# A later load for the last four token tiles, and one z2 tile moved ahead of the second group's q, k chunks

## The chip, the cores and the metric

The kernel runs on one core of a Trainium2 chip. Its time is the device time of one execution in microseconds (us). TensorE (PE) multiplies matrices, VectorE (DVE), ScalarE (ACT) and GpSimd (POOL) work on tiles in the on-chip memory, SyncE (SP) issues transfers. Each engine takes its own list of instructions in order and waits on semaphores for the others.

## The reference

The input x has 2048 tokens of 512 values (bf16). Two branches read the same layer-normed tokens, and their results are added to x.

```
xn = layernorm(x)
# branch A: 32 heads of 16 values; each token attends to itself and the 7 tokens 2, 4, .. 14 places back
q, k, v = split(xn @ wqkv)
attn = softmax(q . k[pos - 2 w] / 4, w = 0..7)
A = (sum_w attn[w] * v[pos - 2 w]) @ wo
# branch B: gated MLP that mixes the tokens
z = gelu(xn @ w_in)            # 1376 columns
z1, z2 = z[:, :688], layernorm(z[:, 688:])
g = w_sp @ z2 + b_sp           # 2048 x 2048 over the tokens
B = (z1 * g) @ w_out
out = x + A + B
```

## The kernel before

The tokens are 16 tiles of 128. Nearly all data stays on chip; the order of the work is written out by hand in two lists of short names, `vec` (VectorE, and what hangs on it) and `ten` (TensorE, and the ScalarE work behind it). `advance` walks through both and calls `do` for each name, after what `needs` demands of the other list. Every engine then works off its own instructions in the order in which `do` made them. DMA issues of SP stand in one queue in the order of the calls.

What the names around the change mean, with the lines of the profile:

- `s` (L184, L185) are the mean and variance of a token tile, `r` (L188, L189) its 1/sigma on GpSimd, `n` (L198) the normed tile on VectorE, `t` (L207) its turn: a transpose by DMA on SP's queue into `xnT`, for tiles 4 to 15. Tiles 0 to 3 are turned on TensorE (`T`, L203).
- `LX` calls `load_tokens`: tokens of tiles 8 to 11 and of tiles 12 to 15, in two transfers (L143) of 512 KB from SP, each behind a memset of one word (L174) that ties its issue to VectorE's place in the list. Tiles 4 to 7 and the weights of q and k were issued before (`LE`).
- `k` with two digits is one of four chunks of q and k for a group of four token tiles (L256 on TensorE, copied by ScalarE at L258): k10, k12, k11 and k13 are those of the second group, tiles 4 to 7, and need the turns t4 to t7.
- `z` (L211) is the matmul of one tile of z2, `h` (L222) its gelu with a running sum on ScalarE, `q` (L227) its sum of squares on ScalarE. A tile z4 or later needs its own turn only.
- `zs` (L233 to L237) makes mean and 1/sigma of z2 for four tiles at once: three small steps on VectorE and then two on GpSimd (L236, and the power -1/2 at L237). `zn` (L243) norms one z2 tile on VectorE.
- `m` and `j` (L291) are products of q with a shifted k on VectorE; m00 is the first half of the first such product and j00 its other half, which needs k13. `f` (L294), `p` (L295) and the fold by DMA `d` (L300) add them up over a head's values, and `S` (L307) ends the sum on TensorE. `K` copies a border of k. `LW` loads the weights of v and z1 from GpSimd's queue.
- `v` (L271) are the values, `W` loads a part of w_sp (L369), `M` (L376) is the token mixing, 512 matmuls in all, and the output products (L414, L420, L426, L563) end the kernel.

The front of `vec` runs tile by tile; from tile 5 on each step is `s r` of a tile and then `n t` of the tile before it:

```
front = "s0 R0 LE s1 R1 V0 n0 V1 n1 s2 r2 s3 r3 n2 n3 LX s4 r4"
for i in range(5, NT):
    front += f" s{i} r{i} n{i - 1} t{i - 1}"
```

The q, k chunks and z2 tiles share three buffers in PSUM (`mm`), taken in turn.

Of the kernel before, what the change touches and what calls it, by code (L numbers as in the profile page):

```python
# [38 lines left out]
def kernel(  # L39
# [13 lines left out]
    V = nc.vector  # L53
# [46 lines left out]
    z2 = z2_r[:].rearrange("p (i f) -> p i f", i=NT)  # L100
# [5 lines left out]
    xs = z1_r[:, 0:NT * D].rearrange("p (i d) -> p i d", i=NT)  # L106
# [10 lines left out]
    def nxt(kind, pool):  # L117
        t = pool[count[kind] % len(pool)]
        count[kind] += 1
        return t  # L120
# [21 lines left out]
    def load_x(i, n=1):  # L142
        SP.dma_start(xs[:, i:i + n, :], x2[i * P:(i + n) * P, :].rearrange("(i p) d -> p i d", p=P))  # L143
# [26 lines left out]

    def load_tokens():

        for i in (8, 12):
            V.memset(xs[:, i, 0:2], 0.0)  # L174
            load_x(i, 4)

    def load_weights():
        G.dma_start(w_v, wq_d[:, :, 2 * D:3 * D])
# [21 lines left out]
    def turn_pe(i):  # L200
        pt = nxt("aux", aux)[:].bitcast(BF16)[:, 0:D]
        for c in range(C):
            PE.transpose(pt[:, c * P:(c + 1) * P], xn[i % 8][:, c * P:(c + 1) * P], ident[:])  # L203
        A.copy(xnT[:, :, i * P:(i + 1) * P], pt.rearrange("p (c t) -> p c t", c=C))  # L204

    def turn_dma(i):
        SP.dma_start_transpose(xnT[:, :, i * P:(i + 1) * P], xn[i % 8])  # L207

    def z_half(i, part, pz, hh):
        for kc in range(C):  # L210
            PE.matmul(pz[:, hh, 0:FHALF], xnT[:, kc, i * P:(i + 1) * P],  # L211
                      w_z2[:, hh, kc] if part else w_z1[:, kc, hh * FHALF:(hh + 1) * FHALF],
                      start=(kc == 0), stop=(kc == C - 1))

    def z_part(i, part):
        pz = nxt("mm", mm)
        for hh in range(2):
            z_half(i, part, pz, hh)
        return pz

    def z2_gelu(i, pz):
        A.activation(z2[:, i, :].rearrange("p (a b) -> p a b", a=2), pz[:, :, 0:FHALF],  # L222
                     ACT.Gelu_apprx_tanh, accum_out=zsum[:, i:i + 1])

    def z2_square(i):

        A.activation(z2_junk[:], z2[:, i, :], ACT.Square, accum_out=zsq[:, i:i + 1])  # L227
# [3 lines left out]
    def z2_stats(i, n):  # L231
        s = slice(i, i + n)
        V.tensor_scalar(zmean[:, s], zsum[:, s], 1.0 / FH, None, ALU.mult)  # L233
        V.tensor_tensor(zvar[:, s], zmean[:, s], zmean[:, s], ALU.mult)
        V.scalar_tensor_tensor(zvar[:, s], zsq[:, s], 1.0 / FH, zvar[:, s], ALU.mult, ALU.subtract)
        G.tensor_scalar(zvar[:, s], zvar[:, s], EPS, 1.0, ALU.add, ALU.mult)  # L236
        G.tensor_tensor(zrstd[:, s], zvar[:, s], mhalf[:, 0:n], ALU.pow)  # L237

    def z2_norm(i, on_act):
        if on_act:  # L240
            A.activation(z2[:, i, :], z2[:, i, :], ACT.Identity, bias=zbias[:, i:i + 1], scale=zrstd[:, i:i + 1])
        else:
            V.tensor_scalar(z2[:, i, :], z2[:, i, :], zmean[:, i:i + 1], zrstd[:, i:i + 1],  # L243
                            ALU.subtract, ALU.mult)
# [5 lines left out]
    def qk_chunks(b, a, c2):  # L250
        pq = nxt("mm", mm)
        t0 = b * D
        for cc in range(2):
            w_c = (w_k if a else w_q).rearrange("p k (o c) -> p k o c", c=C)[:, :, :, 2 * c2 + cc]
            for kc in range(C):
                PE.matmul(pq[:, cc, :], w_c[:, kc], xnT[:, kc, t0:t0 + D], start=(kc == 0), stop=(kc == C - 1))  # L256
        o = HALO + (b % 2) * D
        A.copy(qk[b // 2][:, a, 2 * c2:2 * c2 + 2, o:o + D], pq[:])  # L258
# [16 lines left out]
    def v_halo():  # L275
        G.dma_start(vp[H:P, :, :, 0:HALO], vp[0:P - H, :, :, GS:GS + HALO])
        G.dma_start(vp[0:H, :, 1, 0:HALO], vp[P - H:P, :, 0, GS:GS + HALO])
# [166 lines left out]

    front = "s0 R0 LE s1 R1 V0 n0 V1 n1 s2 r2 s3 r3 n2 n3 LX s4 r4"
    for i in range(5, NT):
        front += f" s{i} r{i} n{i - 1} t{i - 1}"
    front += " n15 t15"
    vec = front.split() + """
        zs0 LW m00 j00 zn0 zn1 zn2 zn3 f00 p00 K m01 d01 m02 d02 zs4 m03 d03 zn4 zn5 zn6 zn7  # L450
        p01 p02 zs8 m10 zn8 zn9 zn10 zn11 p03 W1 f10 zs12 p10 zn12 zn13 zn14 zn15
        m11 d11 g0 x0 m12 d12 p11 g1 u0 m13 p12 W2 W3 f13 p13 c0 g2
        a0.0 a0.1 g3 x1 a0.2 a0.3 g4 a0.4 g5 a0.5 a0.6 a0.7 g6 u1 a0.8 g7 a0.9 g8 a0.10 g9 a0.11 c1 g10
        a1.0 a1.1 g11 a1.2 a1.3 g12 a1.4 g13 a1.5 g14 a1.6 a1.7 g15 X1 a1.8 a1.9 F0 a1.10 a1.11 F1 F2
    """.split()
    ten = """
        T0 T1 GL z0 z1 h0 T3 h1 z2 h2 z3 h3 k00 k01 q0 k02 k03 q1 q2 q3 k10 k12 k11 k13
        W0 k20 z4 h4 q4 k21 z5 h5 q5 k22 z6 h6 q6 k23 z7 h7 q7 k30 z8 h8 q8 k31 z9 h9 q9 S00 v0
        k32 z10 h10 q10 k33 z11 h11 q11 z12 h12 z13 h13 q12 v1 S01 S02 v2 z14 h14 q13 z15 h15 q14 v3
        q15 v4 B S03 y0 y1 M0 S10 v5 v6 EL v7 H e0 M1 EG y2 y3 y4 EL1 i0 EG1 M2 y5 y6 y7 y8 y9 S11 S12 S13 M3 y10 y11 M4 y12  # L460
        M5 W4 W5 y13 y14 y15 O4 EL2 e1 M6 O0 O1 M7 W6 i1 M8 O2 M9 W7 M10 O3 M11 M12 X0 M13 M14 M15 Q0 Q2 Q3
    """.split()
# [115 lines left out]
    def do(n):  # L578
        k, a = n[0], n[1:]
        i = int(a) if a.isdigit() else 0  # L580
        th, w2 = (int(a[0]), int(a[1])) if len(a) == 2 and a.isdigit() else (i, 0)
        if k == "T":
            turn_pe(i)
        elif n[:2] == "zs":
            z2_stats(int(n[2:]), 4)
        elif n[:2] == "zn":
            z2_norm(int(n[2:]), False)
        elif n == "z0":

            gates["z0"], gates["z1"] = nxt("mm", mm), nxt("mm", mm)  # L590
            for t, hh in ((0, 0), (1, 0), (0, 1)):
                z_half(t, 1, gates[f"z{t}"], hh)
        elif n == "z1":
            turn_pe(2)
            z_half(1, 1, gates["z1"], 1)
        elif k == "z":
            gates[n] = z_part(i, 1)
        elif k == "h":
            z2_gelu(i, gates[f"z{i}"])
        elif k == "q":  # L600
            z2_square(i)
        elif k == "k":
            qk_chunks(th, w2 // 2, w2 % 2)
        elif k == "v":
            v_pair(i)
        elif k == "H":
            v_halo()
        elif k == "S":
            head_sum(th, w2)
        elif k == "B":  # L610
            pb = nxt("aux", aux)[:].bitcast(BF16)[:, 0:NT]
            PE.transpose(pb, b16[:], ident[0:NT, 0:NT])
            A.copy(b_col[:], pb)
        elif k == "y":
            z1_tile(i)
        elif k == "M":
            gates[i] = mix_tile(i)
        elif k == "W":
            load_wsp(i)
        elif k == "O":  # L620
            load_wo(i) if i < 4 else load_wout()
        elif k == "X":
            load_res(i)
        elif n == "GL":
            A.preload_act_table(ACT.Gelu_apprx_tanh)
        elif n[:2] == "EG":
            A.preload_act_table(ACT.Gelu_apprx_tanh)
        elif n[:2] == "EL":
            A.preload_act_table_set("natural_log_exp_and_others")
        elif k == "Q":  # L630
            [out_pair, None, lambda: out_group(2), lambda: out_last(3)][i]()
        elif k == "F":
            if i == 0:
                finish_pair(groups[i][0])
                finish_pair(groups[i][2])
            else:
                for t in groups[i]:
                    finish(t, po[t])
        elif k == "e":
            softmax_exp(i)  # L640
        elif k == "i":
            softmax_inv(i)
        elif k == "s":
            ln_stats(i)
        elif k == "R":
            ln_root_act(i, 1)
        elif k == "V":
            ln_inv(i)
        elif n == "LE":
            load_early()  # L650
        elif k == "r":
            ln_root(i, 1)
        elif k == "n":
            ln_norm(i)
        elif k == "t":
            turn_dma(i)
        elif n == "LX":
            load_tokens()
        elif n == "LW":
            load_weights()  # L660
        elif k == "m":
            run(prod_ops(th, w2)[0])
        elif k == "j":
            run(prod_ops(th, w2)[1])
        elif k == "f":
            prod_ops(th, w2)[2]()
        elif k == "p":
            prod_ops(th, w2)[3]()
        elif k == "d":
            fold_dma(th, w2)  # L670
        elif k == "K":
            k_halo()
        elif k == "x":
            run(softmax_max(i))
        elif k == "u":
            run(softmax_sum(i))
        elif k == "c":
            run(softmax_scale(i))
        elif k == "g":
            gate(i, gates[i])  # L680
        elif k == "a":
            at[int(a[0])][int(a[2:])]()
        done.add(n)

    def run(ops):
        for f in ops:
            f()
# [48 lines left out]
```

## Time and profile before

| | |
|---|---|
| median of 3 runs | 202.96 us (202.73 to 204.01) |
| profiled execution | 203.05 us, its span 201.3 us |
| TensorE busy | 194.7 us, 1575 matmuls |
| VectorE busy | 176.1 us |
| ScalarE busy | 95.9 us |
| GpSimd busy | 38.8 us |
| transfers | 30.84 MB, 153 GB/s in the mean |

The span goes from the first to the last instruction that the profile shows; the time holds some 1.8 us around it. A busy share says what an engine does over the whole span; what decides is which engine waits for which at one place, and the chain of work that ended last tells it. In a timeline a row is: start, length, engine, line, operation, output and inputs with their shapes, the count, and in brackets the idle time of the engine before it with what ended it.

### The profile page before, as it was taken

To read this page: it belongs to the slowest core of one execution; us is meant where nothing else is said; L and a number is where in the kernel's file an instruction comes from. 1 tells how busy PE (TensorE), PEld (TensorE's weight loads), DVE (VectorE), ACT (ScalarE), POOL (GpSimd) and SP (SyncE) were. 2 spreads that over 40 slices of the span, in tenths; PEclk is the share of its full clock that TensorE was granted. 3 is DMA by queue.
4 is the path that set the end of the run, shared out by engine and by line. 5 is a ranking of instruction groups with operands and counts; after the bars stand their busy time and mean duration, and the time that the engine had idled before them with its cause. 6 is when DMAs were issued, how large, how long until landed. Compare 5 with 4: busy or idle time off the path is not lost.

```text
span 201.3 us, 3826 instructions
## 1 busy us (share of the span) xinstructions
PE 194.7 (97%) x1575; PEld 117.7 (58%) x1583; DVE 176.1 (87%) x193; ACT 95.9 (48%) x149; POOL 38.8 (19%) x62
## 2 busy tenths in 40 slices
PE   6898999999999999999999999999999999999993
PEld 2554555555666666666566666666666664444652
DVE  4868989999799799999999999989999799897233
ACT  3778869998989349786443165311122110000000
POOL 2355773139460430700000000000000000000000
PEclk9999999999999999999999999999999999999999
DMA  5996649999941939995978099997989411722023
GB/s 143 357 283 113 83 104 211 209 139 218 212 99 26 185 65 142 202 112 121 209 171 170 0 241 299 188 232 128 267 119 273 92 39 40 237 81 100 8 104 104
DMA packets 64353, 30.84 MB, mean 153 GB/s; under 512 B 53504, under 2 KB 62576, under 8 KB 64208
## 3 DMA queue, kind: packets, MB, share of 16 engines
q1 hardware_dynamic: 59808, 19.76, 48.9%
q0 software_dynamic: 1904, 6.59, 17.2%
q10 hardware_dynamic: 2624, 4.25, 8.3%
q8 instruction: 12, 0.20, 0.4%
q14 instruction: 5, 0.04, 0.1%
HBM read 10.03 MB, written 2.10 MB: 60 GB/s over the span
## 4 chain that ended last, share of the span: by engine, by line
PE 89%; DMA 6%; DVE 3%; POOL 1%; issue 1%
PE mm L376 37%; PE mm L211 16%; PE mm L256 10%; PE mm L271 7%; PE mm L414 7%; PE mm L426 5%; DMA z<-in_A_x_dram 4%; PE aux L414 2%; PE mm L563 1%; DVE stats L184 1%; DMA xnT<-z 1%; PE mm L420 1%; PE aux L307 1%; DVE z L198 1%; POOL rstd L189 1%
## 5 line engine op out<-in xcount | busy, mean ns | idle before, releaser
L376 PE MATMUL mm<-z,wsp 128*128 128x344 bf16 x512 | 75.8, 309 | 0.0
L376 PEld LDWEIGHTS <-wsp 128*128 128x128 bf16 x512 | 49.9, 98 | 25.2 <-issue 0.8
L211 PE MATMUL mm<-wts,xnT 128*128 128x344 bf16 x256 | 40.4, 310 | 0.2 <-ACT xnT L204 0.2
L379 ACT ACTIVATE qk<-mm,b_col 128x688 bf16<-128x688 f32 x16 | 13.3, 833 | 50.6 <-PE mm L376 50.6
L349 DVE TENSOR_TENSOR prod<-vp,a_sb 128x4096 bf16<-128x4096 bf16 x16 | 36.1, 2285 | 0.0
L211 PEld LDWEIGHTS <-xnT 128*128 128x128 bf16 x256 | 24.6, 98 | 13.9 <-issue 0.6
L256 PE MATMUL mm<-xnT,wts 128*128 128x512 bf16 x123 | 28.8, 380 | 0.8 <-DMA xnT<-z 0.6
L291 DVE TENSOR_TENSOR prod<-qk 128x4096 bf16<-128x4096 bf16 (+1 forms) x14 | 27.1, 1980 | 0.3 <-PE aux L307 0.3
L353 DVE TENSOR_TENSOR prod<-prod,prod 128x8192 bf16<-128x8192 bf16 x6 | 26.5, 4421 | 0.1
L256 PEld LDWEIGHTS <-wts 128*128 128x128 bf16 x128 | 14.3, 114 | 13.4 <-issue 1.8
L258 ACT CAST qk<-mm 128x1024 bf16<-128x1024 f32 x16 | 16.1, 1011 | 5.2 <-PE mm L256 5.2
L271 PE MATMUL mm<-xnT,wts 128*32 128x512 bf16 x256 | 14.8, 381 | 0.0
L414 PE MATMUL mm<-wts,qk 128*128 128x512 bf16 (+1 forms) x62 | 14.2, 371 | 0.4 <-issue 0.3
L184 DVE BATCH_NORM_STATS2 stats<-z 128x6 f32<-128x512 bf16 x16 | 10.9, 683 | 3.9 <-DMA z<-in_A_x_dram 3.9
L248 ACT ACTIVATE z<-mm 128x688 bf16<-128x688 f32 x16 | 11.8, 743 | 4.8 <-PE mm L211 4.7
L414 PEld LDWEIGHTS <-qk 128*128 128x128 bf16 x85 | 8.1, 98 | 9.2 <-issue 0.6
L431 DVE TENSOR_TENSOR z<-mm,wsp 128x512 bf16<-128x512 f32 (+1 forms) x9 | 5.7, 657 | 8.0 <-PE mm L426 4.8
L227 ACT ACTIVATE z_junk<-z 128x688 bf16<-128x688 bf16 x16 | 12.4, 777 | 0.3
L222 ACT ACTIVATE z<-mm 128x688 bf16<-128x688 f32 x16 | 11.9, 744 | 1.5 <-PE mm L211 1.5
L271 PEld LDWEIGHTS <-wts 128*32 128x32 bf16 x256 | 9.5, 139 | 4.4 <-issue 0.6
L300 POOL DMA_DIRECT2D prod<-prod x8 | 7.1, 928 | 19.4 <-DVE prod L291 19.4
L426 PE MATMUL mm<-wts,xnT 32*128 32x512 bf16 x160 | 10.7, 375 | 0.0
(92 smaller groups left out, 184.6 us busy)
## 6 DMA issues: line engine op xcount, KB each, us to landing
prod<-prod POOLq DMA_DIRECT2D x8, 512.0 KB, 6.9
wts<-in_A_wo_dram ACTq DMA_DIRECT2D x4, 512.0 KB, 5.5
z<-in_A_x_dram SPq DMA_DIRECT2D x3, 512.0 KB, 6.6
out_dram<-z SPq DMA_DIRECT2D x11, 128.0 KB, 1.7
wts<-in_A_wqkv_dram SPq DMA_DIRECT2D x2, 512.0 KB, 6.0
z<-z POOLq DMA_DIRECT2D x2, 512.0 KB, 8.6
wsp<-in_A_x_dram ACTq DMA_DIRECT2D x1, 1024.0 KB, 5.4
wsp<-in_A_x_dram SPq DMA_DIRECT2D x1, 1024.0 KB, 5.3
```

Source lines behind the costliest of these rows:

```text
L184: V.bn_stats(stats[:, i, :], xs[:, i, :])
L211: PE.matmul(pz[:, hh, 0:FHALF], xnT[:, kc, i * P:(i + 1) * P], w_z2[:, hh, kc] if part else w_z1[:, kc, hh * FHALF:(hh + 1) * FHALF], star ...
L256: PE.matmul(pq[:, cc, :], w_c[:, kc], xnT[:, kc, t0:t0 + D], start=(kc == 0), stop=(kc == C - 1))
L258: A.copy(qk[b // 2][:, a, 2 * c2:2 * c2 + 2, o:o + D], pq[:])
L271: PE.matmul(pv[32 * g:32 * g + 32, dd, :], w, r, start=(kc == 0), stop=(kc == C - 1), tile_position=(0, 32 * g))
L291: ops.append(lambda ww=ww, k=k, c=c: V.tensor_tensor(pr[:, ww, c], q[:, c], k[:, c], ALU.mult))
L349: return lambda: V.tensor_tensor(dst, vp[:, :, th, off:off + GS], a_sb[:, th, w].unsqueeze(1).broadcast_to([P, DH, GS]), ALU.mult)
L353: return lambda: V.tensor_tensor(dst, dst, x, ALU.add)
L376: PE.matmul(pg[:, hh, 0:FHALF], w[:, k, (j % 2) * P:(j % 2 + 1) * P], z2[:, k, hh * FHALF:(hh + 1) * FHALF], start=(k == 0), stop=(k == NT ...
L379: A.activation(g.rearrange("p (a b) -> p a b", a=2), pg[:, :, 0:FHALF], ACT.Identity, bias=b_col[:, j:j + 1])
L414: PE.matmul(po[:, cols], uT[th][:, m, t0:t0 + P], wout[:, m, cols], start=(start and m == 0), stop=(stop and m == MF - 1))
L426: PE.matmul(pos[g], op[32 * g:32 * g + 32, th, d, s * P:(s + 1) * P], wo_r[32 * g:32 * g + 32, d, :], start=(start and d == 0), stop=(stop ...
```

## The change

The load of tokens 12 to 15 leaves `load_tokens`, with its memset, and becomes a step of its own, `LZ`, right behind t7 on SP. In `ten`, z4 with its gelu comes between q1 and q2, ahead of k10; the squares q2 and q3 are spread between the chunks, and z5 to z13 stand one place earlier than their forerunners. In `vec`, zn0 to zn3 come ahead of j00.

```diff
     def load_tokens():
-        for i in (8, 12):
-            V.memset(xs[:, i, 0:2], 0.0)
-            load_x(i, 4)
+        V.memset(xs[:, 8, 0:2], 0.0)
+        load_x(8, 4)
...
     for i in range(5, NT):
-        front += f" s{i} r{i} n{i - 1} t{i - 1}"
+
+        front += f" s{i} r{i} n{i - 1} t{i - 1}" + (" LZ" if i == 8 else "")
...
-        zs0 LW m00 j00 zn0 zn1 zn2 zn3 f00 p00 K m01 d01 m02 d02 zs4 m03 d03 zn4 zn5 zn6 zn7
+        zs0 LW m00 zn0 zn1 zn2 zn3 j00 f00 p00 K m01 d01 m02 d02 zs4 m03 d03 zn4 zn5 zn6 zn7
...
-        T0 T1 GL z0 z1 h0 T3 h1 z2 h2 z3 h3 k00 k01 q0 k02 k03 q1 q2 q3 k10 k12 k11 k13
-        W0 k20 z4 h4 q4 k21 z5 h5 q5 k22 z6 h6 q6 k23 z7 h7 q7 k30 z8 h8 q8 k31 z9 h9 q9 S00 v0
-        k32 z10 h10 q10 k33 z11 h11 q11 z12 h12 z13 h13 q12 v1 S01 S02 v2 z14 h14 q13 z15 h15 q14 v3
+        T0 T1 GL z0 z1 h0 T3 h1 z2 h2 z3 h3 k00 k01 q0 k02 k03 q1 z4 h4 q2 k10 k12 q3 k11 k13
+        W0 q4 k20 z5 h5 q5 k21 z6 h6 q6 k22 z7 h7 q7 k23 z8 h8 q8 k30 z9 h9 q9 k31 z10 h10 q10 S00 v0
+        k32 z11 h11 q11 k33 z12 h12 q12 z13 h13 q13 v1 S01 S02 v2 z14 h14 z15 h15 q14 v3
...
+        elif n == "LZ":
+            load_x(12, 4)
```

## The prediction

> **What bounds the kernel now.** The page first, for the busy shares; then the chain of work that ended last, for the places where the end does not hang on TensorE; then the timelines of VectorE and GpSimd from 5 to 67 us, for the slack behind these places.
>
> ```profile
> span 201.3 us, 3826 instructions
> PE 194.7 (97%) x1575; PEld 117.7 (58%) x1583; DVE 176.1 (87%) x193; ACT 95.9 (48%) x149; POOL 38.8 (19%) x62
> ```
>
> TensorE works 97% of the span, its clock row is 9 throughout, and the edit adds and removes no matmul. So the change can only open or close waits of TensorE, of which there are 6.6 us. The chain says which of them matter:
>
> ```profile
> 9.06 6.57 DMA z<-in_A_x_dram
> 15.65 0.70 DVE stats L184
> 16.35 0.02 issue
> 16.38 0.19 DVE mv L185
> 16.57 0.08 issue
> 16.64 0.24 POOL rstd L188
> 16.88 2.33 DMA xnT<-z
> 19.22 0.14 issue
> 19.35 4.27 PE mm L256 x19
> ```
>
> The reader is to see one loop: tokens 8 to 11, issued at 9.06, land at 15.62. Statistics of tile 8 (s8) wait for them, and the norm of tile 7 (n7) stands behind s8 on VectorE. So turn t7 is issued at 16.88 and lands at 19.2, and only then k10 (q, k chunks of the second group) starts. TensorE had finished k03 at 18.76; the waits give "PE mm L256 <- DMA xnT<-z: 0.6". From 19.35 on TensorE has no wait over 0.2 us until the end. **0.6 us is thus all that can be won**; more than that can be lost wherever TensorE comes to wait for a late VectorE.
>
> **Where VectorE could be late.** The head sums S00 to S03 (L307) need its products. Lines of VectorE's timeline, then the TensorE rows that wait for them:
>
> ```profile
> 26.50 4.63 DVE L291 TENSOR_TENSOR prod<-qk 128x2048 bf16<-128x2048 bf16 x4
> 31.05 1.65 DVE L243 TENSOR_SCALAR z<-z,zmean,zrstd 128x688 bf16<-128x688 bf16 x4
> 50.94 1.66 DVE L243 TENSOR_SCALAR z<-z,zmean,zrstd 128x688 bf16<-128x688 bf16 x4 [0.93 <-POOL zrstd L237]
> 52.52 1.21 DVE L295 TENSOR_TENSOR prod<-prod 128x2048 bf16<-128x2048 bf16 x1
> 54.30 1.23 DVE L295 TENSOR_TENSOR z<-z 128x2048 bf16<-128x2048 bf16 x1 [0.57 <-DMA z<-z]
> ```
>
> ```profile
> 55.88 0.39 PE L307 MATMUL aux<-prod,rsel 128*32 128x512 bf16 x4
> 56.10 0.39 PE L307 MATMUL aux<-z,rsel 128*32 128x512 bf16 x4
> ```
>
> p01 and p02 are the last two VectorE rows, S01 and S02 the two of TensorE. p02 ends at 55.53 and S02 starts at 56.10: 0.55 us of slack. In front of p02 VectorE itself idles 0.57 us for a fold transfer. So **VectorE may be 1.1 us late in the stretch before p02; what goes beyond delays S02, and with it all TensorE work behind it**.
>
> **The change, part by part.**
>
> *z2 of tile 4 between q1 and q2.* Eight matmuls (1.17 us in the chain) move into the hole at 18.76; they need only t4, issued at 11.23, landed 6.5 us later at 17.7. TensorE then works until 19.93, past t7's landing at 19.2. Gain 0.6 us. ScalarE does h4 (0.93 us with its read) earlier and q2, q3 later: q3 ends near 25.5 instead of 22.4, and its first reader zs0 starts at 25.95 at the earliest. No cost; the cover is 0.4 us. With later z2 tiles one place up, S00 comes 1.2 us later in TensorE's list, with 7 us of slack to p00 (36.2); in front of S01 and S02 the same tiles are done as before. No cost.
>
> *Load of tokens 12 to 15 behind t7.* One memset (0.04 us) goes. On SP the load (0.41 us of issue) leaves the place in front of t4 and stands between t7 and t8. In front of t4 it delayed nothing that waits: t4 to t6 land at 17.7 to 18.5 now and are needed after 18.76. Does t7 come earlier? It hangs on s8, so on the load of tokens 8 to 11, and the queue works in order: both 512 KB loads were issued 0.44 us apart and landed at 15.62 and 17.1, 1.5 us apart. What stands behind tokens 8 to 11 should not hold them. I take t7 as unchanged, at 16.88.
>
> The new load is then issued at 16.88 + 1.22 (a turn's issue) = 18.1. Nothing shows this load alone. Bounds: 1024 KB of tokens landed in 5.3 us and 256 KB of output in 2.8, so 512 KB alone is about 3.6 us; tokens 4 to 7, beside weight loads, took 4.3. Near t7 and t8 and the instruction fetch of 16 KB there, I take 3.9 between these: landing at 22.0 (21.7 to 22.4). s12 started at 20.17 before without waiting for data. **VectorE is 1.85 us later from s12 on** (1.5 to 2.2). Behind s12 on VectorE stand n11 to n15, zs0 and all products.
>
> The Trainium skill (DMA: Bandwidth & Descriptors, Anatomy of one DMA) states about 2.0 us fixed plus bytes at 436 GB/s: an estimate of 3.2 us here, by which the sum would be 0.7 us less. The trace is against it: for 1024 KB it would make 4.4 us, and 5.3 were measured.
>
> What is late next: t11 needs n11, 1.3 us behind s12's start, so at 23.3; its landing (2.3 to 3.3 us) at 25.6 to 26.6 is in time for k20, which TensorE reaches at 19.93 + 4 x 1.73 = 26.85. t15 is issued at 28.0, before it was 28.3, and the weight transposes behind it on SP keep their place. Turns t8 to t15 cost nothing.
>
> *zn0 to zn3 ahead of j00.* zn0 needs 1/sigma from GpSimd (L236, L237), started by zs0. GpSimd's rows:
>
> ```profile
> 26.67 1.10 POOL L236 TENSOR_SCALAR zvar<-zvar 128x4 f32<-128x4 f32 x1 [1.09 <-DVE zvar L235]
> 27.86 1.88 POOL L237 TENSOR_TENSOR zrstd<-zvar,mhalf 128x4 f32<-128x4 f32 x1
> 47.94 2.96 POOL L237 TENSOR_TENSOR zrstd<-zvar,mhalf 128x4 f32<-128x4 f32 x1
> 56.44 3.07 POOL L237 TENSOR_TENSOR zrstd<-zvar,mhalf 128x4 f32<-128x4 f32 x1
> 67.46 1.01 POOL L237 TENSOR_TENSOR zrstd<-zvar,mhalf 128x4 f32<-128x4 f32 x1
> ```
>
> The powers end 0.9 us after the end of a VectorE product that ran when they began: 29.74 after 28.81, 50.90 after 50.0, 59.51 after 58.57. The one that met no product took 1.01. So in the new order, with m00 (two products of 1.16) started at T, the power ends at T + 2.31 + 0.93 = T + 3.24, as before. j00 hid it, since zn0 came at T + 4.55. Now zn0 comes at T + 2.31 and **VectorE stands 0.96 us**. Bounds: 0.2 if the power needs only its 1.01 from T + 1.4, and 1.2 as before zn12. I take 0.96, since three rows agree. Nothing pays it back: j00's input k13 is in SBUF at about 28.1, and without the swap j00 would start at 30.7 without a wait.
>
> The Trainium skill (SBUF — State Buffer, Who interferes with whom) speaks against this part: a VectorE instruction with two SBUF inputs blocks a GpSimd one that reads SBUF until it is done. By that rule the power can only start when m00 ends, as the rows show; were it free, the sum would be 0.8 us less.
>
> *Sum.* VectorE's delay: 1.85 + 0.96 = 2.8 us. Of it 1.1 is slack, so S02 comes 1.7 us later than before (p02 ends at 57.75, S02 starts at 57.8). The 0.6 us won at 18.76 is not to be taken off again, since TensorE just waits longer at S01 and S02. The fold behind p02 lands at 54.25, limited by transfers that shift with zs0; at 54.25 + 1.85 = 56.1 it is in time for p02 at 56.5. Later needs have room: p03 ends at 63.44, S03 starts at 64.31; p13 at 95.2 against 96.5; the last attention product at 182.7 against 186.2. TensorE is without other waits, so the end moves by 1.7. The profiled execution: 203.05 us with its span of 201.3, against a median of 202.96, so the two agree within 0.1. **203.0 + 1.65 = 204.6 us**; with its own bounds (landing 3.6 to 4.3) 204.2 to 205.0.
>
> **Rivals.**
>
> 1. *Tokens 8 to 11 land sooner without a load behind them: no loss.* What speaks for it: w_k landed at 11.9, 1.4 us behind w_q, and the next 512 KB came 3.7 us later.
>
> ```profile
> 15.50:16.00 0.50, 0.50 (x4) 0.23 (x2) 0.35 (x1) 0.50 (x1) 0.00 (x0) 1.00 0.07 25
> ```
>
> Here the DMA share is 0.07 of 16 engines: one engine alone still brings tokens while 15 are done. If the second load is what holds this one, tokens 8 to 11 land at 13.3; t7 is issued behind t6 at 15.2, the new load at 16.4, landing at 20.0 to 20.7. VectorE is late by -0.15 to 0.5, plus 0.96; less 1.1 of slack that is -0.3 to +0.4: 202.6 to 203.4, taken at 203.0, and 202.4 at best, when nothing is late and the hole closes. Against it: the order in the queue. 25%.
>
> 2. *One DMA engine holds the new load too: clearly slower.* The price is the 2.3 us that tokens 8 to 11 came late (15.6 instead of 13.3), or 1.5 as t9's landing (4.1 against 2.3 to 3.3) suggests; it decides as soon as one sixteenth of the load is late. s12 at 23.5 to 24.3, and TensorE's wait for S02 grows by the same: 206.1 to 207.0. k20 waits too (t11 at 27 to 28), but in the shadow of S02. 20%.
>
> 3. *VectorE's delay meets more slack than I see, or the swap costs only 0.2*: the sum is 0.8 less, 203.8. 10%.
>
> **How the numbers follow.** Forecast 45%, rivals 25, 20 and 10%. A measurement of this kernel tells about 1% from no change: below 200.9 or above 205.0. No case lies below 200.9, as the only hole is 0.6 us; 4% for what I don't see. Above 205.0: rival 2, and the upper edge of the forecast and something of an unseen cost, 33%. Within: 63%. Range 202.4 (best of rival 1) to 206.4 (most of rival 2's lower half); the forecast's own is 204.2 to 205.0.
>
> **What would show it.** Right: k10 without a wait behind z4; s12 with an idle of some 1.8 us for tokens 12 to 15; zn0 with about 0.95 us for GpSimd; no wait for the fold before p02; TensorE waiting at S01 or S02 for VectorE, 2 us in all. Wrong: s8 starting before 15; s12 without a wait; TensorE without a wait at L307.

## The result and the profile after

The changed kernel takes 204.16 us in the median of 16 runs (203.76 to 204.92), the kernel before 202.84 us in 16 (202.16 to 204.38). The ratio is 1.0051, with a 95% interval of 1.003 to 1.0072: slower by half a per cent, 1.0 us by the ratio and 1.3 by the medians. The forecast was 204.6 us. The profiled execution took 204.48 us, against 203.05 before; its span is 1.5 us longer.

From the page of the changed kernel, the span and the busy shares:

```profile
span 202.8 us, 3824 instructions
PE 195.3 (96%) x1575; PEld 118.3 (58%) x1583; DVE 176.1 (87%) x192; ACT 95.9 (47%) x149; POOL 40.7 (20%) x62
```

No engine has more instructions. GpSimd's 62 take 1.9 us more in sum; TensorE's 1575 recorded matmuls add up to 0.6 us more, and its waits grow from 6.6 to 7.5 us. TensorE's timeline, with the hole that was to be filled and the head sums S01, S02 and S03 (a row is start, length, engine, line, operation, and in brackets the wait before it):

```profile
18.88 1.33 PE L210 MATMUL mm<-wts,xnT 128*128 128x344 bf16 x8
20.05 8.80 PE L255 MATMUL mm<-xnT,wts 128*128 128x512 bf16 x39
...
55.98 0.40 PE L306 MATMUL aux<-prod,rsel 128*32 128x512 bf16 x4 [0.48 <-DVE prod L294]
57.11 0.40 PE L306 MATMUL aux<-z,rsel 128*32 128x512 bf16 x4 [0.73 <-DVE z L294]
...
65.73 0.40 PE L306 MATMUL aux<-prod,rsel 128*32 128x512 bf16 x4 [0.33 <-DVE wsp L367]
```

S03 before:

```profile
64.31 0.40 PE L307 MATMUL aux<-prod,rsel 128*32 128x512 bf16 x4
```

z4 stands at 18.88 and k10 follows without a wait: the hole of 0.59 us is gone. But S01 waits 0.48 us, S02 0.73 and S03 0.33, each for VectorE (the last names a memset that ran beside p03; p03's last row is what S03 needs). S02 starts at 57.11 instead of 56.10, S03 at 65.73 instead of 64.31, and from there TensorE runs to the end as before, 1.4 to 1.5 us later.

VectorE's timeline shows what made it late:

```profile
21.19 0.69 DVE L183 BATCH_NORM_STATS2 stats<-z 128x6 f32<-128x512 bf16 x1 [3.14 <-DMA z<-in_A_x_dram]
...
27.42 2.35 DVE L290 TENSOR_TENSOR prod<-qk 128x2048 bf16<-128x2048 bf16 x2
30.68 1.83 DVE L242 TENSOR_SCALAR z<-z,zmean,zrstd 128x688 bf16<-128x688 bf16 x4 [0.91 <-POOL zrstd L236]
...
34.81 2.29 DVE L293 TENSOR_TENSOR prod<-prod 128x4096 bf16<-128x4096 bf16 x1
...
54.72 1.21 DVE L294 TENSOR_TENSOR prod<-prod 128x2048 bf16<-128x2048 bf16 x1
55.85 1.21 DVE L294 TENSOR_TENSOR z<-z 128x2048 bf16<-128x2048 bf16 x1
...
57.55 4.50 DVE L290 TENSOR_TENSOR prod<-qk 128x4096 bf16<-128x4096 bf16 x2
62.98 1.57 DVE L242 TENSOR_SCALAR z<-z,zmean,zrstd 128x688 bf16<-128x688 bf16 x4 [0.93 <-POOL zrstd L236]
```

Of before, f00 and m10:

```profile
32.62 2.28 DVE L294 TENSOR_TENSOR prod<-prod 128x4096 bf16<-128x4096 bf16 x1
...
56.32 4.50 DVE L291 TENSOR_TENSOR prod<-qk 128x4096 bf16<-128x4096 bf16 x2 [0.25 <-PE aux L307]
```

In the changed kernel, first row: s12 waits 3.14 us for tokens 12 to 15 and starts at 21.19, 1.0 us later than before; m00 (27.42 instead of 26.50) is 0.92 us late. Third row: zn0 waits 0.91 us for GpSimd's power, and the four norms take 1.83 us instead of 1.65. From m00's start to f00's (34.81) it is 7.39 us, before 6.12, so the swap costs 1.27. p01 (54.72 instead of 52.52) is the sum of both, 2.2 us late; p02 ends at 57.06 instead of 55.53 and does not wait for a fold as it did before. Last row: a wait of 0.93 us at zn8 that before did not have. GpSimd's row of the power for zs0 and its two rows for zs8, and then the two rows of zs8 before:

```profile
28.77 1.88 POOL L236 TENSOR_TENSOR zrstd<-zvar,mhalf 128x4 f32<-128x4 f32 x1
57.70 2.20 POOL L235 TENSOR_SCALAR zvar<-zvar 128x4 f32<-128x4 f32 x1 [2.77 <-DVE zvar L234]
59.98 2.96 POOL L236 TENSOR_TENSOR zrstd<-zvar,mhalf 128x4 f32<-128x4 f32 x1
```

```profile
56.16 0.20 POOL L236 TENSOR_SCALAR zvar<-zvar 128x4 f32<-128x4 f32 x1 [3.44 <-DVE zvar L235]
56.44 3.07 POOL L237 TENSOR_TENSOR zrstd<-zvar,mhalf 128x4 f32<-128x4 f32 x1
```

Before, m10 had to wait 0.25 us for S01, and in this gap GpSimd's first step took 0.20 us. After, m10 starts at once at 57.55; the step, ready at 57.7, ends with m10's first product at 59.9, and the power 0.9 us behind m10's end.

The chain that ended last has changed accordingly. Some of its longest pieces in order of time (start, length, what):

```profile
16.57 4.60 DMA z<-in_A_x_dram
28.77 1.89 POOL zrstd L236
32.52 2.27 DVE prod L290 x2
42.85 4.40 DVE z L290 x2
47.55 5.91 DMA z<-z
55.93 1.13 DVE z L294
59.98 2.97 POOL zrstd L236
64.55 1.14 DVE prod L294
66.13 2.44 PE mm L210 x16
```

From the load of tokens 12 to 15 to S03 at 65.7 it runs over transfers, VectorE and GpSimd, where before it ran over TensorE from 19.35 on. (The fold at 47.55 stands in the chain, but VectorE shows no wait for it: it worked from 53.13 to p02 without a break, and stood before that for GpSimd's power.)

And the load of tokens 8 to 11, issue to landing, after (first) and before (second):

```profile
z<-in_A_x_dram SPq DMA_DIRECT2D x1, 512.0 KB, 4.3
```

```profile
z<-in_A_x_dram SPq DMA_DIRECT2D x1, 512.0 KB, 6.6
```

Issued at 9.1 in both, it lands at 13.4 instead of 15.6. s8 doesn't wait, t7 is issued 1.6 us sooner, and the new load goes out at 16.57 instead of the forecast 18.1.

### The profile page after: what moved, and what is told of

Its sections match the earlier page's. It is cut to its first block, busy times and chain, and to the rows that moved or that the text cites. A ratio compares the mean times of both kernels' runs of the same rounds, so it can differ in the third digit from the quotient of the medians.

```text
span 202.8 us, 3824 instructions
## 1 busy us (share of the span) xinstructions
PE 195.3 (96%) x1575; PEld 118.3 (58%) x1583; DVE 176.1 (87%) x192; ACT 95.9 (47%) x149; POOL 40.7 (20%) x62
## 4 chain that ended last, share of the span: by engine, by line
PE 66%; DVE 18%; POOL 6%; DMA 6%; issue 1%; SPq 0%; DVEq 0%
PE mm L375 37%; PE mm L210 9%; PE mm L413 7%; PE mm L425 5%; DMA z<-in_A_x_dram 3%; DVE stats L183 3%; DVE prod L290 3%; DMA z<-z 3%; PE mm L270 3%; POOL zrstd L236 2%; DVE z L290 2%; DVE z L242 2%; DVE z L197 2%; PE aux L413 2%; DVE prod L294 2%; POOL rstd L188 2%
## 5 line engine op out<-in xcount | busy, mean ns | idle before, releaser
L299 POOL DMA_DIRECT2D prod<-prod x8 | 7.1, 930 | 20.7 <-DVE prod L290 20.7
```

## The experiments

The theory after the result: VectorE's delays (0.9 us by the late load, 1.3 by the swap of zn0 to zn3 and j00) add up against a slack of some 1.1 us in front of p02; only what goes beyond costs, and S03 pays a little more through GpSimd at zs8. Rivals: one of the parts alone is the loss; or the waits are paid in full. All ratios are to the kernel before, run on the same chip. Executions of one kernel differ by 1 to 2 us at the start and in the transfers; in the profiled executions of `e2_z4` and `e4_noswap` the first twelve z2 matmuls took 3.62 us instead of 1.92, so of these two only the rows of transfers and GpSimd are read.

**One part at a time.** The loads alone:

```diff
-        for i in (8, 12):
-            V.memset(xs[:, i, 0:2], 0.0)
-            load_x(i, 4)
+        V.memset(xs[:, 8, 0:2], 0.0)
+        load_x(8, 4)
...
+        front += f" s{i} r{i} n{i - 1} t{i - 1}" + (" LZ" if i == 8 else "")
```

> Only the loads are changed as in the changed kernel; z4 and the order of zn0 to zn3 are those of before. Theory (only VectorE's lateness beyond about 1.1 us before p02 costs time, and the load and the swap must both be there to exceed it): tokens 8 to 11 land at 13.5, s8 starts without a wait, t7 lands near 17.7, k10 starts at 18.8 without a wait; s12 is 1.0 us late, p02 finds it within its slack. TensorE waits at most 0.4 us at S01 and S02 together: 0.2 to 0.6 us faster than before. Rival A (the late load alone is the loss): about 1 us slower than before. Rival B (tokens 8 to 11 landed early by chance in the profile of the changed kernel): s8 waits to 15.6 again, s12 starts near 22.

202.48 us, ratio 0.9992 (0.9966 to 1.0017). Tokens 8 to 11 landed after 4.6 us; s12 waited 2.42 us and started at 20.59, so only 0.4 us late instead of the 1.0 expected, since the load took 4.2 us. VectorE ended p02 at 55.16, S02 came at 55.21 without a wait, and all that TensorE waited for in the stretch was S03:

```profile
PE aux L306 <- DVE wsp L367: 0.3, 1, 0.3
```

So the late load alone is not the loss: rival A falls, with an upper end of 1.0017 where it wanted about 1.005. Rival B falls too: tokens 8 to 11 came early again. The gain of 0.2 to 0.6 us is not to be told from none by these runs.

TensorE's list alone:

```diff
-        ... k02 k03 q1 q2 q3 k10 k12 k11 k13
-        W0 k20 z4 h4 q4 k21 z5 h5 q5 ...
+        ... k02 k03 q1 z4 h4 q2 k10 k12 q3 k11 k13
+        W0 q4 k20 z5 h5 q5 k21 ...
```

> Only TensorE's list is changed: z4 ahead of the second group's chunks; loads and order of zn0 to zn3 are those of before. Theory: tokens 8 to 11 land at 15.6 as before, since the second load is behind them again; z4 fills the hole at 18.8; p02 is where it was (55.5) and S02 comes at 55.5: 0.5 us faster. Rival C (the changed order of ScalarE's squares or of S00 costs): same as before or slower. If tokens 8 to 11 land near 13.5 here, what held them was not the load behind.

202.54 us, ratio 0.9987 (0.9955 to 1.0019). No loss of more than 0.4 us, but no gain that can be told either: the 0.5 us of the theory and the "same as before" of rival C both lie inside the interval, so this run does not decide between them. Tokens 8 to 11 landed after 4.9 us, between the 4.3 and the 6.6 expected by the two sides.

The swap alone:

```diff
-        zs0 LW m00 j00 zn0 zn1 zn2 zn3 f00
+        zs0 LW m00 zn0 zn1 zn2 zn3 j00 f00
```

> Only zn0 to zn3 are ahead of j00; the rest is that of before. Theory: zn0 waits 0.9 us for GpSimd's power, which p02 finds within its slack of 1.1; but m10 no longer waits for S01, so GpSimd's step at zs8 is locked behind m10's first product (2.2 us instead of 0.2), zn8 waits 0.9 us, and S03 waits 0.2 to 0.4 us: 0.1 to 0.4 us slower. Rival D (every VectorE wait is paid in full): 0.9 us slower. Rival E (the swap is harmless): same, and zn8 without a wait.

203.22 us, ratio 1.0003 (0.9971 to 1.0035). The 0.9 us of rival D would be a ratio of 1.0044, outside the interval. Whether the swap alone costs 0.1 to 0.4 us or nothing stays open (the medians, 203.22 against 202.65, are 0.6 us apart). In its profiled execution, 205.40 us, zn0 waited 0.91 us, zn8 0.93 and S03 0.29, as expected and against rival E; but p02 also waited 2.42 us for its fold, so what the swap alone does at S02 is not seen there.

The change without the swap:

```diff
-        zs0 LW m00 zn0 zn1 zn2 zn3 j00 f00
+        zs0 LW m00 j00 zn0 zn1 zn2 zn3 f00
```

> The changed kernel with j00 back ahead of zn0. Theory: zn0 doesn't wait; VectorE is 1.0 us late by the load alone, S01 and S02 wait 0.4 us together, S03 not at all: 1.0 to 1.4 us faster than the changed kernel, so 0 to 0.4 us faster than before. Rival A (the late load is the loss, the swap is hidden): no more than 0.3 us faster than the changed kernel.

202.53 us, ratio 0.9987 (0.9953 to 1.0021), so 1.3 us faster than the changed kernel by the two ratios (1.0051 - 0.9987, of 202.8 us); rival A wanted 0.3 at the most. The loss needs the swap, and the swap alone, 1.0035 at the most, does not make all of it. This fits the theory that each part is inside the slack and both together are not.

**The load's place as a dose.** Behind t5, t7 (the change) and t8, all else as in the change:

```diff
-        ... + (" LZ" if i == 8 else "")
+        ... + (" LZ" if i == 6 else "")     # f1; i == 9 in f2
```

> The changed kernel with tokens 12 to 15 loaded behind t5 instead of t7 (2.5 us earlier); z4 and the swap of zn0 to zn3 stay. Theory (VectorE's delays add up against a slack of 1.1 us before p02): the load lands near 18.4, s12 waits at most 0.5 us, zs0 starts at 25.6 behind q3; the swap's 0.9 us alone stays within the slack, S01 and S02 don't wait; zn8 waits 0.9 us for GpSimd and S03 0.1 to 0.3 us: 1.0 to 1.5 us faster than the changed kernel, so no more than 0.3 us from before. Rival D (the swap's wait is paid in full, the load was hidden): within 0.4 us of the changed kernel.

203.02 us, ratio 1.0002 (0.9978 to 1.0027): 1.0 us faster than the change. s12 did not wait; zs0 waited for q3, and zn0 the 0.92 us of the swap. The swap is still there and most of its wait is hidden: rival D falls again. S02 waited 0.27 us, though not by VectorE's own lateness: p02 waited 0.61 us for its fold.

> The changed kernel with tokens 12 to 15 loaded behind t8 instead of t7. Theory: the load is issued 1.2 us later (a turn's issue on SP), s12 starts 1.2 us later, and as the slack is used up every microsecond goes into S02: 1.0 to 1.3 us slower than the changed kernel. Rival A' (the load's place is not what counts): within 0.3 us of the changed kernel.

205.56 us, ratio 1.0144 (1.0112 to 1.0175): 1.9 us slower than the change by the two ratios and 1.4 by the medians, more than the 1.0 to 1.3 expected. Rival A' falls. In its profile s12 starts 1.04 us later than in the change and the span is 1.0 us longer. TensorE's waits:

```profile
PE aux L306 <- DVE prod L294: 1.8, 1, 1.8
PE aux L306 <- DVE z L294: 0.7, 1, 0.7
PE aux L306 <- DVE wsp L367: 0.3, 1, 0.3
```

S01's wait grew from 0.48 to 1.8 us, S02's and S03's are the same. In these two profiles a microsecond of VectorE beyond the slack is a microsecond of the kernel; why the runs lie further apart is not shown.

**Can the parts that help be kept?** The load behind t5, without the swap:

```diff
-        ... + (" LZ" if i == 8 else "")
+        ... + (" LZ" if i == 6 else "")
-        zs0 LW m00 zn0 zn1 zn2 zn3 j00 f00
+        zs0 LW m00 j00 zn0 zn1 zn2 zn3 f00
```

> The changed kernel with tokens 12 to 15 behind t5 and j00 back ahead of zn0; only z4's place and the load's are different from before. Theory: VectorE is not late at all (zs0 at 25.6), TensorE has no wait at k10, S01, S02 or S03: 0.1 to 0.5 us faster than before, the most that this hole can give. Rival F (without a hole there is nothing to win, since before has it only in some executions): within 0.1 us of before.

202.82 us, ratio 0.9985 (0.9966 to 1.0004). VectorE was 1 us ahead of before at p01 (51.56), and then waited 1.44 us for the fold in front of p02; the lead was lost there. TensorE's S02 stood at 55.47, 0.6 us ahead of before, but S03 waited 0.33 us, against the expectation, and stood at 64.09, only 0.2 us ahead. The 0.1 to 0.5 us expected and rival F's "no gain" both lie in the interval.

Five of the kernels have z4 ahead of k10 and differ only in the load's place and in the swap:

| ratio to before | load behind t5 | behind t7 | behind t8 |
|---|---|---|---|
| with the swap | 1.0002 | 1.0051 | 1.0144 |
| without | 0.9985 | 0.9987 | not run |

The swap costs 0.3 us with the early load, which these intervals do not tell from nothing, and 1.3 with the late one. Moving the load from t5 to t7 costs 1.0 us with the swap and nothing without.

The same with zs8 one place earlier:

```diff
-        p01 p02 zs8 m10 zn8 zn9 zn10 zn11 p03
+        p01 zs8 p02 m10 zn8 zn9 zn10 zn11 p03
```

> As the kernel with the load behind t5 and without the swap, and zs8 ahead of p02, so that GpSimd's step for z2 tiles 8 to 11 begins before m10. Theory: GpSimd's L235 takes 0.2 to 1.2 us instead of 2.2, the power ends while m10 runs, zn8 doesn't wait, p03 comes up to 0.9 us earlier than with a late zs8; since S03 has slack there, the time stays within 0.2 us of the kernel without this move. Rival G: zs8's three steps (0.45 us) push p02 and S02: 0.3 to 0.5 us slower than it.

202.41 us, ratio 0.9976 (0.9955 to 0.9996): 0.5 us faster than before, and the only version whose interval lies below 1, if barely; among ten versions one may do so by chance. Rival G is not borne out. GpSimd's step took 0.20 us and the power 1.03, and zn8 did not wait. But VectorE stood still for the fold meanwhile, so this shows that the two steps are short with no product beside them, and not that the new place alone makes them so. Its profiled execution, 204.81 us, is one in which the fold came very late:

```profile
56.58 1.23 DVE L294 TENSOR_TENSOR z<-z 128x2048 bf16<-128x2048 bf16 x1 [3.07 <-DMA z<-z]
```

The folds stand behind GpSimd's loads of the weights of v and z1, and the traces differ in when these start against the first transpose of w_sp. Issue to landing in that execution, with the weights issued 0.44 us behind the transpose, and then in the changed kernel, 1.64 us behind it:

```profile
wts<-in_A_wqkv_dram POOLq DMA_DIRECT2D x1, 512.0 KB, 16.0
wsp<-in_B_w_sp_dram SPq DMA_TRANSPOSE x1, 18.9
```

```profile
wts<-in_A_wqkv_dram POOLq DMA_DIRECT2D x1, 512.0 KB, 6.1
wsp<-in_B_w_sp_dram SPq DMA_TRANSPOSE x1, 9.5
```

Two last kernels put the weights behind a memset that follows j00, once on top of the last version, once on the kernel before:

```diff
+        V.memset(w_v[:, 0, 0:2], 0.0)
         G.dma_start(w_v, wq_d[:, :, 2 * D:3 * D])
...
-        zs0 LW m00 j00 zn0
+        zs0 m00 j00 LW zn0
```

> As the kernel with the load behind t5, without the swap and with zs8 ahead of p02; moreover GpSimd's loads of the weights of v and z1 wait for a memset behind j00, some 1.7 us later. Theory H (weight loads that start within 0.5 us of the first w_sp transpose slow both, and the fold behind p02 with them): issued 2 us behind the transpose, w_v lands after 5 to 6 us instead of 16, the transpose after 9 to 10 instead of 19; p02 doesn't wait for the fold, S02 doesn't wait; 201.9 to 202.4 us in the median, 0.2 to 0.5 us faster than without this move, 0.5 to 0.9 us faster than before. Rival I (the fold's lateness in those traces has another cause): p02 waits 1 us or more for the fold as before, the time is the same.

202.35 us, ratio 0.9985 (0.9958 to 1.0012). The weights, issued 1.66 us behind the transpose, landed after 6.6 us and the transpose after 9.4; p02 started at 53.52, right behind zs8, without a wait for the fold. GpSimd's step, now beside p02, took 1.13 us and ended with it; m10 started 0.97 us later than it could have followed p02, the power took 1.03 us and zn8 did not wait. TensorE's waits in the whole span are those of its start:

```profile
PE aux L396 <- DVE wts L158: 1.5, 1, 1.5
PE aux L203 <- DVE z L198: 0.3, 1, 0.3
PE mm L211 <- ACT xnT L204: 0.2, 1, 0.2
```

Theory H holds for the transfers. The gain on the median against the version without the memset, 0.06 us, is not the 0.2 to 0.5 expected: most executions of that version were as fast without it, so the fold cannot often have been as late as in the trace above. Against before it is 0.3 us, not the 0.5 to 0.9 expected, and the interval reaches over 1.

> The kernel before with only this: GpSimd's loads of the weights of v and z1 wait for a memset behind j00, 1.4 us later. Theory H: the first w_sp transpose lands in under 10 us instead of 14, p02 doesn't wait for the fold (0.57 us before), but S02 stands on TensorE's own list, so 0 to 0.4 us faster than before in the median and less spread. Rival I: p02 waits for the fold as before.

203.1 us, ratio 1.0005 (0.9976 to 1.0034). The transpose landed after 9.4 us and p02 did not wait for the fold, as expected; the time is the same, since S02 stands on TensorE's own list there. Of the 0 to 0.4 us of gain expected nothing shows; the interval would not tell 0.4 from nothing.

## Why the prediction was right, and where it was not

*The bound.* Right: 0.6 us at most to be won, any loss through the slack of p02 and S02. In full, though, the 0.6 us is in the profiled execution of before alone; of two other profiles with both token loads together and TensorE's list of before, `g2_before_lw` has a hole of 0.37 us and `e3_swap` none. So the gain of closing it is smaller than the prediction's 0.6 in the mean, and neither the loads alone nor the list alone could be told from no change. Nor was z4 needed to close it: in `e1_loads`, without z4, t7 came early and k10 followed k03 without a wait.

*Tokens 8 to 11 and t7 "unchanged": wrong.* The step that failed is "what stands behind tokens 8 to 11 should not hold them". With the second load behind it this load took 6.6, 4.9, 5.9 and 6.6 us (before, `e2_z4`, `e3_swap`, `g2_before_lw`); without one it took 4.2 to 4.6 us in the profiles of the changed kernel and of the seven others that load tokens 12 to 15 later. This is rival 1's mechanism, and it came with t7 at 15.3 as this rival said. Its result did not come, because the rest of its sum was short: it let the load land at 20.0 to 20.7, and it landed at 21.2; it took 0.96 us for the swap, and it cost 1.27; and it did not have S03.

*Duration of the new load.* Issued at 16.57 it took 4.6 us, above the bounds of 3.6 to 4.3. In the other kernels the same load took 3.6 to 4.4. Both errors together: s12 1.0 us late instead of 1.85. Of the sum's terms this one was sized 0.85 us too large. The fit in the Trainium skill (DMA: Bandwidth & Descriptors, Anatomy of one DMA) is given there for transfers that GpSimd issues, which the prediction does not say; the estimate of 3.2 us from it is for a load from SP's queue, and no such load here took less than 3.6.

*The swap.* The mechanism and the wait were right: 0.91 us at zn0, forecast 0.96, with 1.88 us for the power as before. What was missing is 0.36 us: from the start of zn0 to the next row the four norms take 1.76 us instead of 1.57, and the two halves of the product, no longer one row, take 0.17 more. The part costs 1.27 us. The rule of the Trainium skill (SBUF — State Buffer, Who interferes with whom), that GpSimd is blocked until VectorE's two-input product is done, agrees with the rows here: a first step that met a product ended 0.1 us behind it, and a power 0.9 us; it was this rule that spoke against the change.

*The slack and S02.* Right: p01 is 2.2 us late and S02 1.0, so 1.2 us were slack, 1.1 forecast. `f2_behind_t8` gives the same: p01 at 55.77 is 3.25 us late, S02 at 58.16 is 2.06. The fold was in time, though not at the forecast 56.1: the chain has it in SBUF at 53.5, ahead of before's 54.25, and the weight loads in front of it started 1.64 us behind the w_sp transpose instead of 0.11.

*S03.* Not foreseen: "p03 ends at 63.44, S03 starts at 64.31" was given as room. Once S01 is done when VectorE reaches m10, m10's short wait is gone, and with it the gap in which GpSimd did its first step; 0.93 us at zn8 follow, and 0.33 us at S03. VectorE's lateness is not the only way there: in `e1_loads` and `f3_t5_noswap` TensorE reached S01 0.9 us sooner than before, m10 did not wait, the step took 2.2 us and S03 waited 0.3. So a closed hole alone brings this wait too, and it takes off a part of the gain.

*The sum.* 1.0 at S02 and 0.4 more by S03, against 1.7 forecast at S02 alone. The load's term was 0.85 us too large; the swap's 0.31 and S03's 0.4 were missing. The errors run against each other, so the forecast is nearer to the measured time than its steps were; that nearness is luck. What was not luck is the path: VectorE's two delays, their sum, and the slack that it is taken from.

## What to carry to other kernels

A wait on the path is worth at most its own length, but closing it by moving work costs the slack of every engine that the moved work feeds: sum the delays of one engine up to its next reader and compare the sum, not each part, with the slack there. A transfer that nobody waits for now can become the one that all wait for when it is moved behind others. When steps on two engines contend, hold the order in which they start against each other, not only their lengths.

## What the runs showed of the hardware that was not expected

- A 512 KB load lands later when another 512 KB load is issued 0.4 us behind it on the same queue: 4.9 to 6.6 us in four profiles against 4.2 to 4.6 in eight, although it was issued first. Why it varies was not tested.
- The w_sp transpose and GpSimd's weight loads slow each other when they start within 0.5 us: the transpose takes 14 to 19 us and w_v 6.8 to 16, against 9.2 to 9.8 and 5.3 to 6.6 when the loads start at least 1.5 us later (all profiles, before and after included). Why so little time decides was not tested.
- A GpSimd step that starts 0.15 us behind the start of a product of 2.25 us takes 2.2 us; with no product beside it, 0.2.
